# Window attention and MLP on one core: products of w1 on two engines, half-array transposes for the second chunk, and a fixed order of the first ones

## The chip, the core and the metric

The kernel runs on one core of a Trainium2 chip. The metric is the device time of one execution in microseconds (us): 217.73 as the median of three runs (217.38 to 218.16). A core has TensorE (PE, which loads weights, PEld, and runs matmuls), VectorE (DVE), ScalarE (ACT), GpSimd (POOL) and SyncE (SP), each with an instruction queue of its own that it works off in order, and DMA engines that the queues of POOL, SP and ACT start. PE writes its results to PSUM, from where DVE and ACT evict them to SBUF.

## The reference

Four batches, eight heads, 768 positions, head size 64, model size 512, four sinks and a window of 128.

```python
keep = is_sink | in_window                       # pos < 4, or 0 <= row - col < 128
scores = np.where(keep, q @ k.T / 8, -1e9)
a = exp(scores - max); a = a / (a.sum(-1) + 1e-9)
x = (a @ v), heads side by side                  # (4, 768, 512)
xn = (x - mean) / sqrt(var + 1e-6) * g_ln
out = x + relu(xn @ w_ch1) @ w_ch2               # w_ch1 512x2048, w_ch2 2048x512
```

## The kernel before

The 3072 rows are 24 tiles of 128, two to a chunk, twelve chunks; three chunks make a batch. For each chunk k and q are loaded as bf16, turned so that the head size lies on the partitions (kT, qT), and multiplied to scores (in PSUM, bank pairs `pair`); ACT takes the exponential into `pe`, DVE applies the mask, PE multiplies with v and a column of ones (banks `one`), DVE divides by the sum of that column (`rec`, `x`), takes mean and variance (`bn`, `ag`, tile `st`) and subtracts the mean (`xc`). `xc` is turned into `xnt`. The MLP of a chunk (`mlp`, L1019 to L1080) has eight products `ph` with w1 (relu on ACT or DVE) and eight products `pc` with w2.

The order of the work is not written out. Every piece is an `Op` with a cost per engine, a due time (`prio`) and the buffers it reads, writes and holds; `Plan.run` (L114) places them one by one on the engine that would be done with them first, and hands out the PSUM and SBUF buffers as it goes. What a piece costs in the plan, and which engines it may use, thus decides the order on every engine. Where PE has a gap in the plan within the first 24 us, filler matmuls on constants are put in (L1137). The engines then run their lists, and wait for each other by semaphores.

The places that the change touches:

- **First chunk** (`chunk`, L645 to L680). k and q of the first 256 rows are loaded as f32 in halves of four heads (`natf`), cast to bf16 (`natc`, L663, on DVE or ACT), and turned by four matmuls with the identity each (L671), which write every second column of a PSUM bank; the two rows that a partition holds (index i) thus come out in order of rows. An eviction (L642, `evict`) copies 512 adjoining columns to kT or qT. There are four such groups: k and q of heads 0 to 3, k and q of heads 4 to 7.
- **Second chunk** (`by_pairs`, L578). k and q are loaded as bf16 (`natp`), 256 rows by 8 heads. Each is turned by 32 matmuls on quarters of the array (L599: 64 rows by 64 columns, 64 columns out), into two banks, one for each of the chunk's two tiles; each bank is evicted once, for one tile and all heads. Chunks 2 and 3 use the same function with k and q together (64 matmuls, bank pairs) and stay as they are; later chunks are turned by DMA.
- **Scores of the first tiles** (`attend_tile`, L727). For tiles 0 and 1 PE first writes the mask into the bank (L743), then adds the scores (L763); for tiles 2 and 3 the scores are L722, the sinks L777. An op `sc` waits for the evictions that hold its k and q.
- **Products of w1 with the LN weight** (L1098 to L1101). The first two chunks multiply `xnt` with the LN weight when it is evicted (L900). For the later ones w1 itself is multiplied, in place, when the first two chunks are done with a quarter of it: sixteen pieces of 128 x 512, on DVE.

The four quarters of w1 and of w2 come through POOL's DMA queue (L550, L553), in between the loads of v (L619, L637) and of k and q (L584). The first chunk's MLP has its products by tile (L1030), the others by chunk (L1037); the products with w2 are L1066.

## Time and profile before

| | |
|---|---|
| median of three runs | 217.73 us |
| the profiled execution | 219.54 us |
| its span | 218.0 us |
| mean granted clock of PE | 0.997 |
| busy: PE, PEld, DVE | 206.3, 144.6, 116.9 us |
| busy: ACT, POOL | 105.5, 112.0 us |
| moved by DMA | 28.09 MB, 129 GB/s |

The profile is one execution. Its page gives busy times by engine and by group of instructions and the chain of work that ended last; the trace behind it can be asked for a stretch of time. A line of the timeline reads: start and length in us, engine, line of the kernel, operation, tiles written and read, shapes, count, and in brackets how long the engine sat idle before it and who released it. "Issue" is time in which an engine waited for nothing that the profile shows. A line of the chain of waits has start, length and what it was. In a table of stretches each engine has its busy time and, in brackets, its instructions; the last columns are the clock that was granted to PE, the busy share of the DMA engines and GB/s.

### The profile page before, as it was taken

What the parts mean: (1) busy time and instruction counts of PE and PEld (TensorE: products, weight loads), DVE (VectorE), ACT (ScalarE), POOL (GpSimd) and SP (SyncE); (2) the same over time, 40 slices, a digit from 0 to 9 for tenths busy, and PEclk for the clock granted to TensorE, in tenths of its full rate; (3) what the DMA queues carried; (4) which work ended last, traced back from release to release, by engine and by line L of the source; (5) the groups of instructions that cost most, each with busy time, mean ns of one, the idle gap of its engine ahead of it and who ended that gap; (6) DMA issues with size and microseconds to landing.
All of it is one profiled execution on the core that took longest, in us unless ns stands there. A gap on an engine that the chain in (4) does not pass through costs nothing.

```text
span 218.0 us, 6719 instructions
## 1 busy us (share of the span) xinstructions
PE 206.3 (95%) x2773; PEld 144.6 (66%) x2795; DVE 116.9 (54%) x323; ACT 105.5 (48%) x170; POOL 112.0 (51%) x166
## 2 busy tenths in 40 slices
PE   7797999999999999999999999999999999999991
PEld 2566875664875875874865865865865865856761
DVE  4497875999535536446445456356265265262011
ACT  3785477154571572572562562562652652622600
POOL 7976642589873881871971980971970120120000
PEclk9999999999999999999999999999999999999998
DMA  5999999999999699699799799799999202203011
GB/s 158 185 190 207 192 207 189 161 168 127 200 164 138 116 127 148 83 175 155 123 134 144 117 141 156 105 149 140 110 144 139 75 0 75 72 3 114 6 53 61
DMA packets 104558, 28.09 MB, mean 129 GB/s; under 512 B 94788, under 2 KB 101576, under 8 KB 104520
## 3 DMA queue, kind: packets, MB, share of 16 engines
q0 software_dynamic: 69872, 13.18, 84.2%
q1 hardware_dynamic: 33592, 13.87, 33.3%
q10 hardware_dynamic: 1056, 0.52, 0.9%
q8 instruction: 24, 0.39, 0.8%
q14 instruction: 14, 0.11, 0.2%
HBM read 27.43 MB, written 6.29 MB: 155 GB/s over the span
## 4 chain that ended last, share of the span: by engine, by line
PE 84%; DVE 9%; DMA 2%; issue 2%; ACT 0%; SPq 0%; DVEq 0%
PE one L1066 36%; PE one L1037 34%; PE pair L971 3%; DMA natf<-in_k_dram 2%; PE one L944 2%; PE one L951 2%; PE one L1030 1%; DVE w L1100 1%; DVE st L872 1%; DVE x L864 1%; PE one L960 1%; PE one L979 1%; PE pair L722 1%; PE pair L743 1%; DVE xc L876 1%
## 5 line engine op out<-in xcount | busy, mean ns | idle before, releaser
L1066 PE MATMUL one<-w,h 128*128 128x512 bf16 (+1 forms) x378 | 84.5, 370 | 2.2 <-issue 1.6
L1047 ACT ACTIVATE h<-one 128x512 bf16<-128x512 f32 x93 | 55.6, 598 | 49.7 <-PE one L1037 44.9
L1037 PE MATMUL one<-xnt,w 128*128 128x256 bf16 x704 | 79.3, 273 | 0.0
L1037 PEld LDWEIGHTS <-w 128*128 128x128 bf16 x704 | 68.6, 98 | 10.4
L1066 PEld LDWEIGHTS <-h 128*128 128x128 bf16 x400 | 37.3, 98 | 39.6
L989 ACT ACTIVATE pe<-pair 128x768 bf16<-128x768 f32 x36 | 27.2, 808 | 43.1 <-PE pair L971 43.1
L637 POOL DMA_DIRECT2D vn<-in_v_dram x59 | 38.7, 701 | 9.8 <-DMA w<-in_moe_w_ch_dram 6.8
L881 POOL TENSOR_SCALAR st<-st 128x1 f32<-128x1 f32 x24 | 8.9, 371 | 65.5 <-DVE st L874 65.1
L1012 DVE RECIPROCAL rec<-one 128x4 f32<-128x4 f32 x36 | 6.4, 177 | 62.0 <-PE one L960 50.6
L1074 DVE SCALAR_TENSOR_TENSOR ot<-one,st,x 128x512 f32<-128x512 f32 (+1 forms) x25 | 18.1, 726 | 12.9 <-PE one L1066 7.9
L882 POOL TENSOR_TENSOR st<-st,mhalf 128x1 f32<-128x1 f32 x24 | 17.0, 707 | 2.0
L872 DVE BATCH_NORM_STATS2 st<-x 128x6 f32<-128x512 bf16 x24 | 16.7, 694 | 0.8
L1014 DVE TENSOR_TENSOR x<-one,rec 128x256 bf16<-128x256 f32 x36 | 15.3, 424 | 1.2
L695 POOL DMA_DIRECT2D nat<-in_k_dram x16 | 14.9, 933 | 1.7 <-DMA natp<-in_q_dram 1.0
L695 POOL DMA_DIRECT2D nat<-in_q_dram x16 | 14.3, 907 | 0.0
L994 DVE TENSOR_TENSOR pe<-pe,band 128x768 bf16<-128x768 bf16 x24 | 12.2, 551 | 0.0
L1030 PE MATMUL one<-xnt,w 128*128 128x128 bf16 x128 | 8.3, 219 | 1.3 <-issue 1.0
L876 DVE TENSOR_SCALAR xc<-x,st 128x512 bf16<-128x512 bf16 x24 | 9.0, 374 | 0.9
L971 PE MATMUL pair<-qT,kT 64*64 64x128 bf16 (+1 forms) x528 | 9.2, 204 | 0.0
L944 PEld LDWEIGHTS <-pe 128*128 128x128 bf16 (+1 forms) x144 | 6.3, 97 | 3.3 <-DVE pe L994 0.8
L1030 PEld LDWEIGHTS <-w 128*128 128x128 bf16 x128 | 7.4, 98 | 1.6 <-issue 1.4
L769 ACT ACTIVATE pe<-pair 128x1024 bf16<-128x1024 f32 (+1 forms) x8 | 7.1, 916 | 2.5 <-PE pair L722 2.0
(109 smaller groups left out, 163.0 us busy)
## 6 DMA issues: line engine op xcount, KB each, us to landing
out_dram<-ot SPq DMA_DIRECT2D x23, 256.0 KB
w<-in_moe_w_ch_dram POOLq DMA_DIRECT2D x8, 512.0 KB, 14.4
nat<-in_k_dram POOLq DMA_DIRECT2D x16, 128.0 KB, 4.5
nat<-in_q_dram POOLq DMA_DIRECT2D x16, 128.0 KB, 5.7
vn<-in_v_dram POOLq DMA_DIRECT2D x44, 32.0 KB, 5.6
vn<-in_v_dram POOLq DMA_DIRECT2D x15, 64.0 KB, 5.8
natp<-in_k_dram POOLq DMA_DIRECT2D x3, 256.0 KB, 14.3
vn<-in_v_dram POOLq DMA_DIRECT2D x6, 128.0 KB, 9.6
```

What stands on the lines that cost most here:

```text
L637: P.op(f"vld{t}_{i}", {"POOL": (0.8, 0.85)}, prio + 0.001 * i, lambda e, p0=p0, n=n, hs=hs, src=src: G.dma_start(m.t[p0:p0 + n, hs, 0:64], ...
L695: lambda e, nat=nat, ap=ap: G.dma_start(nat.t, ap), writes=[nat], dma=SW, after=gate(c))
L872: P.op(f"bn{t}", {"DVE": fix(0.60)}, d + 0.12, lambda e: V.bn_stats(st.t[:, 8:14], x.t), reads=[x], writes=[st, mv])
L882: G.tensor_tensor(st.t[:, 16:17], st.t[:, 17:18], mhalf, op=ALU.pow)),
L971: nc.tensor.matmul(pps[u].t[64 * g:64 * g + 64, h2, col + c0:col + c0 + n], lhsT=kt.t[rs, hp, k0:k0 + 64], rhs=qT.t[rs, hp, q0:q0 + n], st ...
L989: nc.scalar.activation(pes[j].t.rearrange("p a b -> p (a b)")[:, 0:768].rearrange("p (a b) -> p a b", a=2), pps[j].t[:, :, 0:384], AF.Exp, ...
L1014: P.op(f"x{t - 1}{u}", {"DVE": dve(256)}, d + 0.051 + 0.002 * u, lambda e, u=u, rc=rc, pv=pv: V.tensor_tensor(x.t[:, 256 * u:256 * u + 256 ...
L1030: nc.tensor.matmul(ph.t[:, 128 * s:128 * s + 128], lhsT=w1[u // 2][:, j, 128 * s:128 * s + 128], rhs=xnt.t[:, j, 128 * (u % 2):128 * (u % ...
L1037: nc.tensor.matmul(ph.t[:, 256 * s:256 * s + 256], lhsT=w1[ht // 4][:, j, 128 * (ht % 4):128 * (ht % 4 + 1)], rhs=xnt.t[:, j, :], start=j ...
L1047: nc.scalar.activation(hb.t, ph.t, AF.Relu)
L1066: nc.tensor.matmul(pc.t[:, 0:wd], lhsT=(h1[2 * s + i].t[:, 128 * ii:128 * ii + 128] if by_tile else h1[ht // 2].t[:, 256 * (ht % 2) + 128 ...
L1074: V.scalar_tensor_tensor(ot.t[:, sl], in0=pc.t[:, 0:wd], scalar=st.t[:, 16:17], in1=x.t[:, sl], op0=ALU.mult, op1=ALU.add),
```

## The change

Four edits. (1) The first chunk's transposes write adjoining columns of the bank (one block of 128 for each i), and the eviction reads with a stride to bring rows into order; their planned cost goes from 0.3 to 0.23. (2) The second chunk's k and q (`whole`) are turned by 16 matmuls on half the array (128 rows by 64 columns, 128 columns out); the two banks now hold heads 0 to 3 and heads 4 to 7 of both tiles, an eviction is for four heads and both tiles, and `tile_of` says so; planned cost 0.45 instead of 0.28. The sink scores wait for both halves of q. (3) The scores of tile 0's first half wait until the last of the four transposes is issued, and the scores of tile 1's first half until those of tile 0's second half are. (4) The sixteen products of w1 and the LN weight may run on ACT too.

The lists of instructions of the two kernels show what follows from it. POOL and SP keep theirs. On ACT and DVE eight products of w1 each: of the four of a quarter, DVE has 3, 1, 1 and 3 and ACT 1, 3, 3 and 1; those of the second quarter that ACT has stand before the relu of the second chunk's fifth product, the others between relus and evictions up to the first exponential of the second batch. All four casts of the first chunk are on ACT, and three of the four evictions on DVE (before: two casts and three evictions on ACT). On PE the first scores stand behind the fourth group of transposes, tile 0's second half before tile 1's first; the products of tile 0 with v stand ahead of a mask; one product with w1 of the first chunk stands behind half of tile 3's product with v; there are five more fillers ahead of the second chunk's transposes and two fewer later. PE has 58 instructions fewer. Elsewhere only the numbers of PSUM buffers are permuted.

```diff
@@ -562,7 +562,7 @@
     xnt_b = [Buf(f"xnt{c}", "xnt") for c in range(NC)]
     xnt_t = [Buf(f"xnt_t{t}") for t in range(NT)]
 
-    tile_of, scores, trs = {}, {}, {}
+    tile_of, scores, scored, trs = {}, {}, {}, {}
 
     def early(t):
         return 0.5 + 0.8 * t
@@ -577,7 +577,7 @@
 
     def by_pairs(c, what, d):
         b, R = c // RC, c % RC
-        nats, pts = [], []
+        nats, pts, whole = [], [], len(what) == 1
         for nm, src, T, ld in what:
             nat = Buf(f"{nm}n{c}", "natp")
             ap = src[b, :, 256 * R:256 * R + 256, :].rearrange("h (p i) d -> p h (i d)", i=2)
@@ -593,24 +593,31 @@
             for nat, pt in zip(nats, pts):
                 for hp in range(HP):
                     for i in range(2):
+                        for h2 in range(2) if whole else ():
+                            nc.tensor.matmul(pt[hp // 2].t[64 * h2:64 * h2 + 64, 256 * (hp % 2) + 128 * i:256 * (hp % 2) + 128 * i + 128],
+                                             lhsT=nat.t[:, 2 * hp + h2, i, :], rhs=ident, start=True, stop=True, skip_group_check=True)
+                        if whole:
+                            continue
                         for h2 in range(2):
                             for r in range(2):
                                 rs, cs = slice(64 * r, 64 * r + 64), slice(64 * h2, 64 * h2 + 64)
                                 nc.tensor.matmul(half(pt, r)[cs, hp, i, :], lhsT=nat.t[rs, 2 * hp + h2, i, :],
                                                  rhs=ident[rs, rs], start=True, stop=True, skip_group_check=True)
-        o = P.op(f"tr{what[0][0]}{c}", pe(0.28 * len(what)), d, tr, reads=nats + [Bc["ident"]], hold=[w[2] for w in what],
-                 writes=[x for pt in pts for x in pt], mode="q")
+        o = P.op(f"tr{what[0][0]}{c}", pe(0.45 if whole else 0.28 * len(what)), d, tr, reads=nats + [Bc["ident"]], hold=[w[2] for w in what],
+                 writes=[x for pt in pts for x in pt], mode="h" if whole else "q")
         for (nm, src, T, ld), pt in zip(what, pts):
             for r in range(2):
                 t, done = 2 * c + r, Buf(f"{nm}T{2 * c + r}")
                 if c == 1:
                     trs[t] = [o]
                 evict(f"ev{nm}{t}", d + 0.05 + 0.02 * r, 512,
-                      lambda pt=pt, r=r: half(pt, r).rearrange("p h i m -> p h m i"),
-                      lambda T=T, r=r: T.t[:, :, 128 * r:128 * r + 128].rearrange("p h (m i) -> p h m i", i=2),
+                      lambda pt=pt, r=r: pt[r].t.rearrange("p (h i m) -> p h m i", h=2, i=2) if whole else
+                      half(pt, r).rearrange("p h i m -> p h m i"),
+                      lambda T=T, r=r: (T.t[:, 2 * r:2 * r + 2, :] if whole else T.t[:, :, 128 * r:128 * r + 128]
+                                        ).rearrange("p h (m i) -> p h m i", i=2),
                       [pt[-1 if len(pt) == 1 else r]], [T, done], fp=True)
                 for hh in range(2):
-                    tile_of[nm, t, hh] = done
+                    tile_of[(nm, 2 * c + hh, r) if whole else (nm, t, hh)] = done
 
     def load_v(t, prio):
         b, r = t // RB, t % RB
@@ -665,16 +672,16 @@
                              reads=[part], hold=[src], writes=[nat])
 
                         def tr(e, pt=pt, nat=nat):
-                            pb = pt.t.rearrange("p (h m i) -> p h m i", h=2, i=2)
+                            pb = pt.t.rearrange("p (h i m) -> p h i m", h=2, i=2)
                             for hp in range(2):
                                 for i in range(2):
-                                    nc.tensor.matmul(pb[:, hp, :, i], lhsT=nat.t[:, i, 2 * hp:2 * hp + 2, :], rhs=ident,
+                                    nc.tensor.matmul(pb[:, hp, i, :], lhsT=nat.t[:, i, 2 * hp:2 * hp + 2, :], rhs=ident,
                                                      start=hp + i == 0, stop=True, skip_group_check=True)
-                        o = P.op(f"tr{nm}{hh}", pe(0.3), d + 0.02 + 0.01 * hh, tr, reads=[nat, Bc["ident"]], hold=[T], writes=[pt])
+                        o = P.op(f"tr{nm}{hh}", pe(0.23), d + 0.02 + 0.01 * hh, tr, reads=[nat, Bc["ident"]], hold=[T], writes=[pt])
                         trs[0], trs[1] = trs.get(0, [o]), [o]
                         evict(f"ev{nm}0{hh}", d + 0.05 + 0.01 * hh, 512,
-                              lambda pt=pt: pt.t.rearrange("p (h c) -> p h c", h=2),
-                              lambda T=T, hh=hh: T.t[:, 2 * hh:2 * hh + 2, :], [pt], [T, done], fp=True)
+                              lambda pt=pt: pt.t.rearrange("p (h i m) -> p h m i", h=2, i=2),
+                              lambda T=T, hh=hh: T.t[:, 2 * hh:2 * hh + 2, :].rearrange("p h (m i) -> p h m i", i=2), [pt], [T, done], fp=True)
                         for t in range(2):
                             tile_of[nm, t, hh] = done
             else:
@@ -763,7 +770,8 @@
                             nc.tensor.matmul(pp.t[:, h2, col:col + 128], lhsT=kt.t[rs, hp, ks], rhs=qT.t[rs, hp, own],
                                              start=t >= PAR["pm"] and col == 0, stop=True, skip_group_check=True)
             done = Buf(f"sd{t}{j}")
-            P.op(f"sc{t}_{j}", pe(0.2 if t > 1 else 0.25 if t else 0.13), d + 0.1 + 0.1 * j, sc, reads=need[j], **(
+            first = trs[1] if (t, j) == (0, 0) else [scored[0, 1]] if (t, j) == (1, 0) else []
+            scored[t, j] = P.op(f"sc{t}_{j}", pe(0.2 if t > 1 else 0.25 if t else 0.13), d + 0.1 + 0.1 * j, sc, reads=need[j], after=first, **(
                 {"rw": [pp], "writes": [done]} if t < PAR["pm"] else {"writes": [pp, done]}),
                  hold=[kT, qT, kprev, pb], mode="q" if t > 1 else "r")
             P.op(f"ex{t}_{j}", {"ACT": act(1024 if t else 512)}, d + 0.11 + 0.1 * j, lambda e, pp=pp, pb=pb, at_j=at_j: nc.scalar.activation(
@@ -776,7 +784,7 @@
                 for hp in range(HP):
                     nc.tensor.matmul(pp_s.t[32 * hp:32 * hp + 32, 0:128], lhsT=kts_b[0].t[:, hp, :],
                                      rhs=qT.t[:, hp, own], start=True, stop=True, skip_group_check=True)
-            P.op(f"sk{t}", pe(0.21), d + 0.15, sk, reads=[tile_of["q", t, 0], kts_b[0]], writes=[pp_s], hold=[qT, ps], mode="c")
+            P.op(f"sk{t}", pe(0.21), d + 0.15, sk, reads=[tile_of["q", t, 0], tile_of["q", t, 1], kts_b[0]], writes=[pp_s], hold=[qT, ps], mode="c")
             P.op(f"sx{t}", {"ACT": act(128)}, d + 0.16, lambda e: nc.scalar.activation(
                 ps.t[:, own], pp_s.t[:, 0:128], AF.Exp, scale=scale), reads=[pp_s], writes=[ps])
 
@@ -1096,8 +1104,9 @@
         if c == PAR["x_by_dma"] - 1:
             for s in range(4):
                 for j in range(NDM):
-                    P.op(f"w1g{s}{j}", {"DVE": fix(0.26)}, 16.0 * c + PAR["w1g"] + 2 * s + 0.1 * j,
-                         lambda e, s=s, j=j: V.tensor_scalar_mul(w1[s][:, j, :], w1[s][:, j, :], gt[:, j:j + 1]),
+                    P.op(f"w1g{s}{j}", {"DVE": fix(0.26), "ACT": act(512)}, 16.0 * c + PAR["w1g"] + 2 * s + 0.1 * j,
+                         lambda e, s=s, j=j: V.tensor_scalar_mul(w1[s][:, j, :], w1[s][:, j, :], gt[:, j:j + 1]) if e == "DVE" else
+                         nc.scalar.mul(w1[s][:, j, :], w1[s][:, j, :], gt[:, j:j + 1]),
                          reads=[Bw1[s], Bc["gt"]], writes=[Bw1g[s]], after=last_use[s])
 
     def guard(e):
```

## The prediction

> **What bounds the kernel now.** Durations come from one profiled execution of 219.54 us: a span of 218.0 and 1.54 around it. The runs shown have a median of 217.73 (217.38 to 218.16), 1.81 lower, so I work out a difference in span and take it off the median. The table of stretches comes first (busy time and count of each engine per stretch), because it says where TensorE (PE) is not full; above it stands the page's line of totals.
>
> ```profile
> PE 206.3 (95%) x2773; PEld 144.6 (66%) x2795; DVE 116.9 (54%) x323; ACT 105.5 (48%) x170; POOL 112.0 (51%) x166
> ```
> ```profile
> core 0: us, PE busy (x) PEld busy (x) DVE busy (x) ACT busy (x) POOL busy (x), PEclk, DMA share, GB/s
> 0.00:16.46 16.46, 13.69 (x222) 7.68 (x222) 10.50 (x44) 11.12 (x18) 13.77 (x22) 1.00 1.36 178
> 16.46:17.50 1.04, 0.00 (x0) 0.00 (x0) 0.46 (x2) 1.00 (x2) 1.04 (x3) 1.00 1.25 205
> 17.50:26.25 8.75, 7.85 (x147) 7.11 (x147) 7.88 (x19) 3.89 (x6) 5.28 (x9) 1.00 1.43 198
> 26.25:53.00 26.75, 26.21 (x401) 17.31 (x404) 21.87 (x67) 14.04 (x24) 15.91 (x24) 1.00 1.46 173
> 53.00:214.00 161.00, 158.59 (x2010) 112.47 (x2022) 76.08 (x193) 75.47 (x122) 75.95 (x112) 1.00 1.15 114
> ```
> From 53 to 214 us PE is 98% busy at full clock; the change touches no work there, and the two instruction lists agree there on every engine but for the numbers of PSUM buffers. So the end moves by what PE gains before 53 us. Three places can give: the head up to 26 us, the 1.04 us in which PE ran nothing, and the half microsecond missing in 26 to 53. The chain of waits, in order of time, names what stood there:
>
> ```profile
> 6.58 0.95 DVE natc L663
> 7.58 0.61 PE one L671 x4
> ...
> 9.47 1.03 ACT pe L769
> ...
> 15.62 0.83 PE one L1030 x13
> 16.46 1.05 issue
> ...
> 17.95 0.69 DVE h L1049
> ...
> 25.68 0.53 DVE xc L876
> ...
> 26.25 0.40 PE one L889 x4
> ```
> Up to 16.5 us the chain hops between casts, transposes, exponentials and normalisation. From 17.95 to 26.2 it is VectorE's queue (DVE) in one run of 8.3 us: from the first relu, through normalising tiles 1 to 3, to the last x minus mean; PE's transpose at 26.25 waits for that. What started the run late is the stop of 1.05 us, with three matmuls of the first w1 product still to come.
>
> **First chunk (dense transposes, their order).** Rows of the timeline:
>
> ```profile
> 4.86 1.14 ACT L663 CAST natc<-natf 128x512 bf16<-128x512 f32 x2 [1.21 <-DMA natf<-in_k_dram]
> ...
> 8.23 0.58 ACT L642 CAST kT<-one 128x512 bf16<-128x512 f32 x1 [0.91 <-PE one L671]
> ...
> 8.99 0.69 DVE L642 CAST qT<-one 128x512 bf16<-128x512 f32 x1 [1.14 <-PE one L671]
> ...
> 10.54 0.69 DVE L642 CAST kT<-one 128x512 bf16<-128x512 f32 x1 [0.53 <-PE one L599]
> ...
> 11.30 0.18 DVE L862 RECIPROCAL rec<-one 128x4 f32<-128x4 f32 x1
> ...
> 13.88 0.40 PE L889 MATMUL one<-ident,xc 128*128 128x128 bf16 x4
> ...
> 14.21 0.24 PE L777 MATMUL one<-qT,kts 128*32 128x128 bf16 x4
> ```
> The new list puts all four casts on ScalarE (ACT) and three of the four evictions on DVE. The third cast starts at 6.58, when its data lands, and takes some 0.6 (1.14 for two) where DVE's took 0.95: the third transpose starts at 7.25, not 7.58. Four transposes into every second column take 0.61; four into adjoining columns (L889) take 0.40, and I take that for the dense ones. The fourth cast ends near 7.75, its transposes near 8.2, and ACT's eviction (0.58) near 8.8, where before DVE's ended at 8.99 + 0.69 = 9.68: 0.9 earlier. The eviction now reads with a stride. L642's evictions of the second chunk (10.54 among them) do so already, at 0.69 on DVE as at 8.99: nothing.
>
> The wait that holds the first scores back until all four transposes are issued starts them at 8.1 as before (in the old list they stood just before the fourth group), for their k and q are evicted by 7.4 (two of 0.69 on DVE, behind transposes done near 5.9). Behind the waiting scores on PE stand only the gain's transpose and fillers. The second half of tile 0 now precedes tile 1, so tile 1's exponential starts 0.25 later than 9.47, but ACT is through all three at 10.75, not 10.98. The five fillers added here stand where PE waits for a cast or an eviction anyway.
>
> **Second chunk (half-array matmuls).** 32 matmuls of 64x64 take 0.45 to the last result (10.04 to 10.49); 16 of 64x128 replace them, for k and for q. No row has a stationary of 128 rows by 64 columns. Bounds: one after the other at the 0.06 that a 128-column matmul steps by (15.62 above, 13 in 0.83) they cost 16 x 0.06 + 0.2 for the last to come through = 1.15; four beside each other like the quarter-array matmuls of L777 (0.24 for all four), 4 x 0.06 + 0.2 = 0.45. I take pairs side by side, 8 x 0.06 + 0.2 = 0.7: 0.25 more, twice. In exchange DVE is free for k's first half at 9.7 instead of 10.54, so the reciprocal of 11.30 starts at 10.4 (0.9 earlier). The second time the q tile's landing and ACT's queue leave less: tile 1's x minus mean ends near 16.2 instead of 16.96. I carry **0.75** for the head, with 0 and 0.9 as ends (serial matmuls cost 0.45 twice, nearly all of it).
>
> **The stop at 16.46.** Nothing that PE reads was missing: the 13 matmuls before it use the same tiles. The instruction queue is the one thing that fits:
>
> ```profile
> 17.50 0.17 PEld L1030 LDWEIGHTS <-w 128*128 128x128 bf16 x3 [1.22 <-issue]
> 17.50 0.34 PE L1030 MATMUL one<-xnt,w 128*128 128x128 bf16 x3 [1.05 <-issue]
> ```
> ```profile
> q8 instruction: 1, 0.02, 5.3%
> ```
> PE stopped after 222 loads and 222 matmuls (first stretch above). Of the DMA view's windows, the one from 15.1 to 16.2 has the one packet shown of queue 8 (16 KB); those from 12.4 to 15.1 and 16.2 to 21.1 have none. So I read it as PE having run out of instructions until a block arrived. The change leaves the data loads' order alone but takes 56 instructions from PE ahead of this point: in the new list instruction 444 is no longer inside the first w1 product but in the second half of tile 3's scores, which I put at 17.45. If the block comes at 17.50 as before, the stop is gone: **1.05** off the chain, and even a late block would stop PE beside DVE's run.
>
> The Trainium skill, "Runtime: NRT & Kernel Launch", section "Instruction fetch mechanics", says that an engine's sequencer fetches the next block of 256 instructions while it executes the current one, and that this is mostly hidden; this speaks against a stop of this size, and is my first rival.
>
> **What caps both.** 0.75 + 1.05 = 1.80 at the first relu meets loads that do not move. Issues of w1 and w2 (DMA view, one row each for the windows 9.9:10.0, 15.1:16.2 and 16.56:17.2), and PE's uses:
>
> ```profile
> w<-in_moe_w_ch_dram POOLq DMA_DIRECT2D x1, 512.0 KB, 15.0
> ```
> ```profile
> w<-in_moe_w_ch_dram POOLq DMA_DIRECT2D x1, 512.0 KB, 14.4
> ```
> ```profile
> w<-in_moe_w_ch_dram POOLq DMA_DIRECT2D x1, 512.0 KB, 16.1
> ```
> ```profile
> 26.49 1.95 PE L1030 MATMUL one<-xnt,w 128*128 128x128 bf16 x32
> ...
> 31.64 1.03 PE L1066 MATMUL one<-w,h 128*128 128x512 bf16 x3
> ...
> 33.29 2.76 PE L1066 MATMUL one<-w,h 128*128 128x512 bf16 x12
> ```
> The last quarter of w1 lands at 9.9 + 15.0 = 24.9 and is used at 26.49; the first of w2 at 15.7 + 14.4 = 30.1, used at 31.64; the second at 16.5 + 16.1 = 32.6, used by the third group of four, 33.29 + 4 x 0.23 (2.76 for 12) = 34.2. Slack is 1.5 each time. Tile 3's part of DVE's run also waits for PE, so I bring it in 1.4 earlier: **1.4** at 26.25, not 1.8.
>
> **Products of w1.** Chain of waits, and rows of the timeline:
>
> ```profile
> 48.83 2.23 DVE w L1100 x6
> ...
> 51.13 0.70 DVE w L1100 x2
> 51.82 0.94 DVE pe L994 x2
> ```
> ```profile
> 40.13 0.60 ACT L1047 ACTIVATE h<-one 128x512 bf16<-128x512 f32 x1 [1.79 <-PE one L1037]
> ...
> 49.48 1.51 ACT L989 ACTIVATE pe<-pair 128x768 bf16<-128x768 f32 x2 [1.54 <-PE pair L971]
> ...
> 52.34 0.20 PE L944 MATMUL one<-vn,pe 64*128 64x65 bf16 x1
> ...
> 52.81 0.30 PE L944 MATMUL one<-vn,pe 64*128 64x65 bf16 x7 [0.27 <-DVE pe L994]
> ```
> Eight products stand in front of the masks for which PE waits at 52.34 to 52.81. The new list has four there on DVE, so the masks come 1.5 earlier, bound then by ACT's exponentials (done near 51): the wait goes, **0.4**. ACT takes eight of the sixteen, at most 0.6 each (its cast of the same size), 4.8 in the 12.7 that it is idle between 26.25 and 53. Three of them stand right before the relu of 40.13, which it otherwise reaches with 1.79 to spare, so nothing is priced there; without that cover each holds the relu, and at worst PE, back by up to 0.6. Next late after the masks is nothing: PE is then full.
>
> **Sum**: 1.4 + 0.4 = 1.8 off the span, 218.0 to 216.2; from the median, **215.9**.
>
> **Rivals.** (1) The stop stays with the w1 product, because it was no missing instruction block: the relu gains 0.75 to 0.85, less than the loads allow, and with 0.4 that is 1.2: 216.5. This is the case that the Trainium skill speaks for on its page "Runtime: NRT & Kernel Launch". For it: no row names a releaser. Against: the one packet just before PE resumes. Chance 0.16. (2) The head's gain is lost in the loads: were the w quarters to land 1.4 later than here, or the half-array matmuls serial and the block late, only the 0.4 is left: 217.3. For it: a slack of 1.5 on three loads in a row; against: their issues are untouched. Chance 0.10. (3) Slower, by this row of the page's list of queues:
>
> ```profile
> q8 instruction: 24, 0.39, 0.8%
> ```
> PE, ahead of its instruction stream, stops at the next two blocks too: with 24 packets for its 5568 instructions a block is about 230, so near instructions 670 and 900. Each stop like the one seen costs 1.05 and falls where PE is the bound; the first has moved and not gone. That is 0.75 + 0.4 gained and 2.1 lost: 218.7. It decides if PE comes to those instructions before the block's packet plus the 1.4 us that the first took. For it, PE is 1.4 us earlier; against it, each block begins some 56 instructions later in the work. Chance 0.08.
>
> **How the numbers follow.** The forecast has 0.66. Its own ends: 2.5 off (head 0.9, loads earlier, 215.2) and 1.3 off (serial matmuls, 216.4). With rival 1 and 0.4 for a part of its wait kept, the range is 215.2 to 216.9, leaving out rivals 2 and 3 (0.18). A difference of 0.3% (0.65 us) is about what a measurement of this kernel can tell from none: faster 0.66 + 0.16 = 0.82, same 0.10, slower 0.08.
>
> **What would show it.** Right: the first w1 product in one piece, its relu near 16.3; no empty 1.04 us of PE before 26 us, or one beside busy DVE; the last w1 product of the first chunk near 25.1; no wait for the masks near 51; the second chunk's 16 transposes within 0.7. Wrong: an issue wait of a microsecond in a w1 product, PE waiting for w near 25, 30 or 33, or ACT's products ahead of a relu for which PE waits.

## The result, and the profile after

Lines of the changed kernel stand 7 to 8 below those of before (L889 is L897, L1030 is L1038, L1037 is L1045, L1066 is L1074, L1078 is L1086, L944 is L952, L994 is L1002; the half-array transposes are L597).

| | before | after |
|---|---|---|
| median of 21 runs each | 218.69 us (217.38 to 219.80) | 217.62 us (216.47 to 218.42) |
| ratio, 95% interval | | 0.9939 (0.9918 to 0.9959) |
| the same two, once more (35 and 12 runs) | 218.61 | 217.84, ratio 0.9971 (0.9947 to 0.9995) |
| profiled execution, span | 219.54, 218.0 | 217.13, 215.5 |

By the two ratios the change makes the kernel 0.3 to 0.6% faster (0.6 to 1.3 us); 0.83% (1.8 of 217.73) was forecast. The forecast of 215.9, range 215.2 to 216.9, did not hold the time. A part of that is its base: the three runs shown before had a median of 217.73, the 21 runs 218.69. Taken off the longer base, 1.8 would have given 216.9, still below 217.62: the gain itself was put too high as well.

The table of stretches of the changed kernel, to be held against the first one of before (busy time and count of each engine, then PE's clock):

```profile
0.00:16.46 16.46, 13.38 (x197) 7.68 (x197) 11.13 (x45) 11.29 (x18) 13.54 (x22) 1.00 1.36 178
16.46:17.50 1.04, 0.67 (x14) 0.66 (x15) 1.04 (x3) 0.81 (x2) 1.04 (x3) 1.00 1.25 205
17.50:26.25 8.75, 8.24 (x157) 7.50 (x154) 7.77 (x22) 3.98 (x7) 5.72 (x10) 1.00 1.43 198
26.25:53.00 26.75, 26.75 (x430) 17.01 (x428) 20.40 (x62) 19.70 (x33) 16.13 (x25) 1.00 1.56 178
```

PE works in the stretch that was empty, and from 26.25 to 53 it is full (26.75 of 26.75, before 26.21), while ACT has 5.7 us more and DVE 1.5 less. The chain of waits of the changed kernel, from the first MLP on:

```profile
14.20 0.69 DVE xnt L908
...
16.42 0.35 DVE xc L884
16.77 0.52 DVE h L1057
...
24.50 0.37 DVE xc L884
...
24.91 0.40 PE one L897 x4
```

The stop is gone from the chain; it now runs through DVE's queue without a break, and the relu (`h`) waits behind tile 1's x minus mean (`xc`), no longer for PE. Tile 3's transposes start at 24.91 instead of 26.25. Near 53 us stands the first w1 product of the third chunk, the first that needs the multiplied w1 (the expectations below call it the second chunk's). Its rows in the timelines of before and after:

```profile
55.37 0.82 PE L1037 MATMUL one<-xnt,w 128*128 128x256 bf16 x6
```
```profile
53.52 0.71 PE L1045 MATMUL one<-xnt,w 128*128 128x256 bf16 x5
```

It comes 1.85 us earlier, and the last `ot` of the kernel starts 1.86 earlier too (211.80 against 213.66). So these two profiles agree with the sum of 1.8, and the runs do not. Two profiles are two draws; the experiments show what was drawn.

### The profile page after: what moved, and what is told of

Its sections match the earlier page's. It is cut to its first block, busy times and chain, and to the rows that moved or that the text cites. A ratio compares the mean times of both kernels' runs of the same rounds, so it can differ in the third digit from the quotient of the medians.

```text
span 215.5 us, 6681 instructions
## 1 busy us (share of the span) xinstructions
PE 207.7 (96%) x2766; PEld 144.2 (67%) x2766; DVE 114.7 (53%) x315; ACT 110.0 (51%) x178; POOL 111.4 (52%) x166
## 4 chain that ended last, share of the span: by engine, by line
PE 89%; DVE 5%; DMA 2%; ACT 1%; issue 1%; SPq 0%; DVEq 0%
PE one L1074 40%; PE one L1045 36%; PE pair L979 3%; DMA natf<-in_k_dram 2%; PE one L952 2%; PE one L959 2%; PE one L968 1%; DVE st L880 1%; DVE xnt L908 1%; PE one L987 1%; PE one L1038 1%; DVE x L872 1%; PE pair L604 1%; PE pair L729 1%; DVE pe L780 1%
## 5 line engine op out<-in xcount | busy, mean ns | idle before, releaser
L1074 PE MATMUL one<-w,h 128*128 128x512 bf16 (+1 forms) x400 | 87.4, 371 | 0.0
L1045 PE MATMUL one<-xnt,w 128*128 128x256 bf16 x704 | 79.3, 273 | 0.0
L1045 PEld LDWEIGHTS <-w 128*128 128x128 bf16 x704 | 68.6, 98 | 10.4
L1074 PEld LDWEIGHTS <-h 128*128 128x128 bf16 x400 | 37.3, 98 | 39.6
L889 POOL TENSOR_SCALAR st<-st 128x1 f32<-128x1 f32 x24 | 8.5, 355 | 61.8 <-DVE st L882 61.2
L1022 DVE TENSOR_TENSOR x<-one,rec 128x256 bf16<-128x256 f32 x36 | 15.3, 425 | 1.2
L1002 DVE TENSOR_TENSOR pe<-pe,band 128x768 bf16<-128x768 bf16 x24 | 12.2, 551 | 0.0
L884 DVE TENSOR_SCALAR xc<-x,st 128x512 bf16<-128x512 bf16 x24 | 8.5, 353 | 0.9
L952 PEld LDWEIGHTS <-pe 128*128 128x128 bf16 (+1 forms) x144 | 6.2, 97 | 2.9 <-issue 0.8
L1038 PE MATMUL one<-xnt,w 128*128 128x128 bf16 x128 | 8.1, 219 | 0.0
L979 PEld LDWEIGHTS <-kT 64*64 64x64 bf16 x528 | 7.2, 108 | 0.4 <-ACT w L1109 0.4
```

The source lines that it names most:

```text
L979: nc.tensor.matmul(pps[u].t[64 * g:64 * g + 64, h2, col + c0:col + c0 + n], lhsT=kt.t[rs, hp, k0:k0 + 64], rhs=qT.t[rs, hp, q0:q0 + n], st ...
L1002: V.tensor_mul(at_s, at_s, band[j] if r > 1 else edge[r][j].unsqueeze(1).to_broadcast([128, 4, 192]))
L1022: P.op(f"x{t - 1}{u}", {"DVE": dve(256)}, d + 0.051 + 0.002 * u, lambda e, u=u, rc=rc, pv=pv: V.tensor_tensor(x.t[:, 256 * u:256 * u + 256 ...
L1045: nc.tensor.matmul(ph.t[:, 256 * s:256 * s + 256], lhsT=w1[ht // 4][:, j, 128 * (ht % 4):128 * (ht % 4 + 1)], rhs=xnt.t[:, j, :], start=j ...
L1074: nc.tensor.matmul(pc.t[:, 0:wd], lhsT=(h1[2 * s + i].t[:, 128 * ii:128 * ii + 128] if by_tile else h1[ht // 2].t[:, 256 * (ht % 2) + 128 ...
```

## The experiments

All ratios are to the kernel before, run beside on the same chip, with their 95% intervals.

**The two kernels again, unchanged.** For before:

> The kernel before, unchanged, for a second profile and more times. Theory A (PE runs out of instructions at its 444th and waits for a block): the stop of about 1.05 us stands again after 222 loads and 222 matmuls, at 16.2 to 17.5 us, with the packet of queue 8 before it. Theory B (the stop belongs to the first w1 product, by chance or by its data): another place or length, or none. Theory C (the times of one kernel fall into two groups about 1.2 us apart because the stop is there in some executions only): no stop if this execution's time is 218.4 or less, a stop if it is above 219. Ratio to the kernel before 1.00.

> The kernel before, unchanged, for a third profile. New theory: TensorE stops after 222 loads and 222 matmuls, until 5.4 to 5.9 us after it passed its 188th instruction, whatever the length of the stop that this gives (1.04 and 0.22 so far). Ratio 1.000.

Ratios 0.9988 (0.9962 to 1.0015) and 1.0002 (0.9976 to 1.0029). Their chains of waits where PE stops, b_again first:

```profile
15.68 0.83 PE one L1030 x13
16.51 0.22 issue
16.74 0.35 PE one L1030 x3
```
```profile
15.22 0.83 PE one L1030 x13
16.05 0.44 issue
16.49 0.35 PE one L1030 x3
```

The place is the same to the matmul, the length is not: 1.05, 0.22 and 0.44 us (and 0.93 in only_w1 below, whose PE does the same work up to there). Tile 3's transposes start at 26.25, 25.33 and 25.07. The profile that the forecast was worked out from had the longest of the three stops.

The changed kernel again:

> The changed kernel once more, for a second profile of it. If the 1.85 us between the two traces at 53 us is what the change is worth, its second chunk's first w1 product starts at 53.5 again; that of before, taken twice, was 55.37 and 54.60, the difference being the length of the stop (1.04 and 0.22). Ratio 0.994.

Its third chunk's first w1 product starts at 53.67, tile 3's transposes at 25.08. Over three profiles of before (55.37, 54.60, 54.36: mean 54.78) and two of after (mean 53.60) the gain there is 1.18 us, 0.54% of 218.6. That lies between the two measured ratios.

**Half-array matmuls alone, and cut in two.**

```diff
+                        for h2 in range(2) if whole else ():
+                            nc.tensor.matmul(pt[hp // 2].t[64 * h2:64 * h2 + 64, ...128 columns], lhsT=nat.t[:, 2 * hp + h2, i, :], rhs=ident, ...)
```
```diff
+                        for cc in (0, 64) if whole else ():
+                            for h2 in range(2):
+                                nc.tensor.matmul(...64 columns, rhs=ident[:, cc:cc + 64], ...)
```

> The kernel before with the half-array transposes of the second chunk alone: 64 instructions fewer on PE and two or so more fillers' worth, so that instruction 444 lies in the scores of tile 3. A: no empty microsecond in the first w1 product; the relu of that product near 16.8 instead of 17.95, the third tile's transpose near 25.2 instead of 26.25, ratio 0.995. B: the stop stays in the first w1 product, ratio 1.000 to 1.002 (0.2 us lost in each transposition).

> As only_half, but each half-array matmul of 128 columns in two of 64 columns: same work, same plan and order, 64 more instructions on PE ahead of the first w1 product, so that instruction 444 is again its 14th matmul. A: the stop is back there, about 1 us, until about 17.5; ratio 1.000, 1.0 us slower than only_half. B: as only_half to 0.2 us.

only_half: 0.9952 (0.9923 to 0.9981), no stop, tile 3's transposes at 24.86. half_split: 1.0005 (0.9977 to 1.0034), with the stop back; its chain of waits:

```profile
15.36 0.89 PE one L1039 x14
16.25 0.64 issue
16.89 0.27 PE one L1039 x2
```

The same work in 64 more instructions, and the gain is gone. What the half-array matmuls bring is their number. They also bring all that was gained ahead of tile 3: no_w1 (below), which has edits 1 and 3 besides, has tile 3's transposes at 24.89, no earlier than only_half's 24.86.

**First chunk's edits alone** (dense transposes and the fixed order, edits 1 and 3):

```diff
-                            pb = pt.t.rearrange("p (h m i) -> p h m i", h=2, i=2)
+                            pb = pt.t.rearrange("p (h i m) -> p h i m", h=2, i=2)
...
+            first = trs[1] if (t, j) == (0, 0) else [scored[0, 1]] if (t, j) == (1, 0) else []
```

> The kernel before with the dense first transposes and their fixed order alone (quarter-array transposes and w1 products on VectorE as before). Instruction 444 is the tenth matmul of the first w1 product. A: the head up to the second tile's x minus mean comes 0.4 to 0.8 earlier, but PE stops in the first w1 product until about 17.5 as before, so the relu gains 0.2 at most and the ratio is 0.998 to 1.000. B: the whole head's gain arrives, ratio 0.997.

0.9987 (0.9960 to 1.0014). Tile 0's transposes are 0.39 earlier than in before's profile (13.49 against 13.88; b_third, unchanged, has 13.47), and PE then waits longer at the same count. Its chain:

```profile
15.23 0.67 PE one L1031 x10
15.90 1.26 issue
17.15 0.51 PE one L1031 x6
```

**Products of w1 alone, and the change without them.**

```diff
-                    P.op(f"w1g{s}{j}", {"DVE": fix(0.26)}, ...
+                    P.op(f"w1g{s}{j}", {"DVE": fix(0.26), "ACT": act(512)}, ...
```

> The kernel before with the products of w1 and the gain also on ScalarE, nothing else. Theory A (the stop goes with the count of TensorE's instructions, and the products are a gain of their own): the stop after 222 loads and 222 matmuls stays in the first w1 product, 0.2 to 1.3 us long; the wait for the masks near 52 (0.4 us) is gone; ratio to before 0.998 (0.4 of 218.6). Rival B (the products cost ScalarE what they save VectorE): a wait before a relu near 40 us takes the place of the masks' wait, ratio 1.000.

> The changed kernel without the products on ScalarE (edits 1 to 3). Theory A with the products worth 0.4: the wait for the masks is back near 51 and the second chunk's first w1 product starts 0.4 later than in the changed kernel (53.9 against 53.52); ratio to before 0.996. Rival B: products worth nothing, ratio 0.994.

0.9982 (0.9957 to 1.0007) and 0.9967 (0.9934 to 1.0000). The products with v for which the masks had been late, in the timelines of only_w1 and of no_w1:

```profile
52.00 0.30 PE L944 MATMUL one<-vn,pe 64*128 64x65 bf16 x8
```
```profile
51.37 0.20 PE L952 MATMUL one<-vn,pe 64*128 64x65 bf16 x1 [0.29 <-DVE pe L1002]
51.83 0.17 PEld L952 LDWEIGHTS <-pe 64*128 64x128 bf16 x7 [0.38 <-DVE pe L1002]
51.84 0.30 PE L952 MATMUL one<-vn,pe 64*128 64x65 bf16 x7 [0.27 <-DVE pe L1002]
```

With the products shared, eight run in one piece; without them PE waits twice. The intervals can't tell 0.4 from nothing, the traces can: from tile 3's transposes to the third chunk's first w1 product it is 28.60 to 28.73 us in the eight profiles with products on ACT (mean 28.63), and 29.05 to 29.51 in the nine without (mean 29.26). The products are worth **0.63**, more than the 0.4 that the expectations had.

**Is it the count?** Two kernels that move the 444th instruction and nothing else: before without its five later fillers, and the changed kernel with its five first fillers cut in eight.

```diff
-        if n > 0 and room > 0.3:
+        if n > 0 and room > 0.3 and cold:
```
```diff
                 for i in range(-s):
-                    nc.tensor.matmul(o[1][:, 0:o[0]], lhsT=junk[:, 0:128], rhs=junk[:, 0:o[0]], ...)
+                    for p in range(8 if o[0] == 512 else 1):
+                        cols = slice(64 * p, 64 * p + 64) if o[0] == 512 else slice(0, o[0])
+                        nc.tensor.matmul(o[1][:, cols], lhsT=junk[:, 0:128], rhs=junk[:, cols], ...)
```

> The kernel before without its five filler matmuls after 5.6 us (10 instructions fewer on TensorE, no other work touched). The first w1 product has then ended 4 instructions before the 444th, which is in tile 1's transposes. Theory A (TensorE runs out of instructions at the 444th): the w1 product is in one piece and its relu near 16.7, and tile 1's transposes are what stops, until 16.8 to 17.5; ratio 0.996 to 0.999. Rival C (something in the w1 product itself holds TensorE there, such as its weights): the product stops with three matmuls left, as before, and the ratio is 0.999 to 1.000.

> The changed kernel with its five first filler matmuls of 512 columns each cut in eight of 64 (35 matmuls and 35 loads more at 1 to 3 us, where TensorE waits for the first data; everything behind them unchanged). The 444th instruction is then in the first w1 product again. Theory A: a stop of 0.2 to 1.3 us inside the first w1 product, tile 3's transposes 0.3 to 1.1 later than in the changed kernel (24.91), ratio to before 0.996 to 0.999. Rival D (the half-array matmuls gain by themselves, and the stop is of another kind): no stop, tile 3's transposes near 24.9, ratio 0.994.

> The kernel of a_fill8 once more, whose profile had a granted clock of 0.85 from 5 to 16.2 us. At full clock the first w1 product starts near 15.4 and TensorE comes to its 444th instruction after 6 of the 16 matmuls, near 15.8. Theory A: it stops there until 16.7 to 17.5, as in the other kernels, 0.9 to 1.7 us; ratio 0.995 to 0.998. Rival D: no stop; ratio 0.994.

b_less: the w1 product is in one piece, and PE pauses between the second and the third of tile 1's transposes, again behind 222 loads and 222 matmuls:

```profile
16.63 0.28 PE one L889 x2
16.92 0.13 issue
17.05 0.30 PE one L889 x2
```

The time, though, is 219.83, ratio 1.0061 (1.0029 to 1.0093), which neither theory had; more of it below. a_fill8: 0.9951 (0.9927 to 0.9975), and a_fill8_b, the same kernel at full clock, 0.9954 (0.9931 to 0.9977). In a_fill8_b 222 loads and 222 matmuls end ahead of the seventh load of the first w1 product, and nothing stops there:

```profile
15.32 1.07 PE L1038 MATMUL one<-xnt,w 128*128 128x128 bf16 x16
16.70 0.40 PE L897 MATMUL one<-ident,xc 128*128 128x128 bf16 x4 [0.31 <-DVE xc L884]
```

So the theory that the place in the list decides fell. What differs is when the packet of queue 8 came. The DMA view of a_fill8_b from 12.9 to 13.2 us, and that of the changed kernel from 15.1 to 15.3:

```profile
q8 instruction: 1, 0.02, 19.5%
```
```profile
q8 instruction: 1, 0.02, 29.5%
```

The 70 early instructions brought it two microseconds forward (13.06 against 15.19), and PE's 95th load as much (9.90 against 12.00). New theory: the block is asked for when PE is 256 instructions ahead of it (the 188th, its 95th load), takes a fixed time to come, and PE stops if it runs through the 256 faster. Two further runs, with the 256 in other work:

> The changed kernel with each half-array matmul cut in two of 64 columns (64 matmuls and loads more, same work). Its 188th instruction is then in tile 1's scores, near 11.2 us, and its 444th in the first w1 product after 9 matmuls, near 16.0: 4.8 us for 256 instructions. New theory (the block comes 5.4 to 5.9 after the 188th): a stop there of 0.6 to 1.1 us, resumed 16.6 to 17.1, tile 3's transposes near 25.4 instead of 24.91, ratio to before 0.996 to 0.999. Rival (neither place nor pace, a_fill8_b's missing stop being chance): no stop or one of any length, with no relation to 5.4 to 5.9 us.

> The kernel before with its five first filler matmuls each cut in eight of 64 columns (70 instructions more at 1 to 3 us, nothing else). Its 188th instruction is then in the first group of quarter-array transposes, near 10.1, and its 444th in tile 3's first scores, near 15.1 with no stop. New theory: the block comes at 10.1 + 5.4 to 5.9 = 15.5 to 16.0, so TensorE stops 0.4 to 0.9 us in those scores, and the first w1 product, now in one piece, ends near 17.0 instead of 17.86; ratio 0.996 to 1.000. Rival (the stop belongs to the w1 product): it stays there, with three matmuls left.

after_split is the changed kernel with the cut of half_split; b_fill8 is before with the cut fillers. Ratios 0.9984 (0.9958 to 1.0010) and 0.9982 (0.9954 to 1.0010). Their chains of waits, after_split first:

```profile
15.45 0.67 PE one L1040 x10
16.12 0.35 issue
16.47 0.51 PE one L1040 x6
```
```profile
14.38 0.29 PE pair L722 x14
14.67 0.64 issue
15.31 0.39 PE pair L722 x18
15.71 0.17 PE one L777 x4
15.88 1.01 PE one L1030 x16
```

In b_fill8 the stop has left the w1 product and stands in tile 3's scores, where the 444th instruction then is; the product is in one piece. after_split stopped 0.35, less than the 0.6 expected. Over all 17 profiles (packet times and counts of loads are from the trace's own records; the stop stands behind 444 to 446 instructions):

| | PE's 95th load to the first instruction of the block | packet on queue 8 to that instruction |
|---|---|---|
| nine that stop (before, b_again, b_third, only_w1, only_dense, half_split, b_less, b_fill8, after_split) | 5.35 to 6.13 us | 2.28 to 2.50 us |
| eight that don't (after, a_again, only_half, no_w1, a_less, w2_late, a_fill8, a_fill8_b) | 5.71 to 6.12 us | 2.54 to 3.11 us |

In the first row PE was there after 4.8 to 5.9 us and waited; in the second its own work took as long as the block, and no kernel got an instruction earlier than 2.28 us after the packet. That PE asks in steps of 256 the later packets show too: in all 17 profiles the first four came 2.7 to 3.9 us after PE's 95th, 223rd, 351st and 479th load, which are 128 loads and 128 matmuls apart (the second counted from the load behind the stop, where there is one). The time to come is not fixed, though: b_third's block came 0.43 sooner after the 95th load than before's (5.41 against 5.84), and its stop is shorter for that. The table also tells why b_again stopped so shortly: its load of q was late (a wait of 0.69 at 12.05, below), PE lost that time inside the 256, and got it back at the stop. What sets the 5.4 to 6.1 us was not tried; the DMA share in the tables of stretches is above 1.2 all that time.

**Where the head's gain went.** The changed kernel without its last five fillers, and the same with w2's loads issued later by POOL:

```diff
-        if n > 0 and room > 0.3:
+        if n > 0 and room > 0.3 and o.start < 9.5:
```
```diff
-    items = [(o.start, o.seq, o) for o in order]
+    late = {"w2ld0": 2.8, "w2ld1": 2.8, "w2ld2": 2.8, "w2ld3": 0.9}
+    items = [(o.start + late.get(o.name, 0.0), o.seq, o) for o in order]
```

> The changed kernel without the filler matmuls behind 9.5 us (two of 256 columns at 11.48, three more after the first w1 product). Theory E (in the changed kernel TensorE's own queue is the bound from 9.3 to 13.7, which is where the head's gain went): tile 0's transposes start at 13.4 instead of 13.69, tile 1's x minus mean ends 0.3 earlier than 16.77, ratio to before 0.9925. Rival F (VectorE's queue or the landing of the q load is the bound): tile 0's transposes stay at 13.6 to 13.7 or their copy at 14.2, ratio 0.994.

> The run a_less with the loads of w2's quarters issued by GpSimd behind tile 1's statistics instead of before (first issue near 16.9 instead of 15.76); every other engine's list is the same. Theory G (tile 1's x minus mean on VectorE is held while GpSimd begins to issue those loads): x minus mean starts near 16.1 as in a_less and takes 0.35 instead of 0.57, so it ends at 16.5, 0.2 earlier, and so do the relu and tile 3's transposes (24.65). Rival H (it is held by something else, or the relu by the first w1 product's end at 16.2): it ends at 16.7 again, tile 3's transposes at 24.86. The quarters of w2 land about a microsecond later, so the ratio is left open: 0.994 if PE has enough work before them, up to 0.998 if it waits for them near 30.

Ratios 0.9944 (0.9920 to 0.9968) and 0.9950 (0.9923 to 0.9977): neither beats the changed kernel. In a_less tile 0's transposes come at 13.41, as theory E had it, but tile 3's only at 24.86 (24.91). Its timeline, DVE and POOL, and then that of w2_late:

```profile
16.14 0.57 DVE L884 TENSOR_SCALAR xc<-x,st 128x512 bf16<-128x512 bf16 x1
...
15.76 2.36 POOL L553 DMA_DIRECT2D w<-in_moe_w_ch_dram  x3
```
```profile
16.25 0.35 DVE L884 TENSOR_SCALAR xc<-x,st 128x512 bf16<-128x512 bf16 x1
...
17.27 2.35 POOL L553 DMA_DIRECT2D w<-in_moe_w_ch_dram  x3
```

The x minus mean that begins 0.38 after POOL's first issue takes 0.57; with the issue behind it, it takes 0.35, as theory G had it. The other profiles make the pattern plain. In the first 60 us of all 17, an x minus mean takes 0.35 when it begins less than 0.2 us or more than 0.6 after POOL began to issue a load, but for one (in a_fill8, 0.92 beside a TENSOR_TENSOR of POOL). Of the 33 in between 30 are stretched, and 26 of them end 0.95 to 0.99 us after POOL began, whenever they started: for tile 1, b_third (begun 0.33 after, takes 0.63), b_less (0.44, 0.52), only_dense (0.48, 0.47), b_again (0.53, 0.42). So it is held until some 0.6 us after POOL's start, and what comes earlier in that window gains nothing. The Trainium skill ("SBUF — State Buffer", "Who interferes with whom") has such a rule: VectorE's tensor_scalar can take a port pair that it shares with GpSimd, and the later of the two blocks fully; the stretched rows agree, with 0.07 to 0.28 us lost by tile 1's. By the Trainium skill the first one keeps the pair for its whole instruction, and there the rows differ: POOL's issue of w2 takes 0.75, but holds an x minus mean until 0.6 only. w2_late's tile 3 is only 0.11 earlier than a_less's, half of what was expected, because its tile 0 was itself 0.12 later. Nor did w2 land later: its second quarter, issued 1.51 later than in a_less, landed at 32.46 (32.48).

**The end of the kernel.** b_less had its last `ot` at 212.58, 1.08 earlier than before, and yet ends later (span 218.4). In the trace's own records two of PE's last three instructions, parts of the final barrier, stand at 216.70 and 218.12, with a packet of queue 8 that began at 215.73, 2.39 before the second; in the other 16 profiles they are 0.15 to 0.20 apart. It fits that ten instructions fewer have moved the end of a block between them; no further run tests that. The end also varies by itself. From the end of the last `ot` to the end of the span it is 3.90, 4.22 and 3.17 us in the three profiles of before, so the second, with a stop of only 0.22, still took 219.09: the time of an execution does not tell whether PE stopped, and theory C of b_again fell. A part of it is SP's: the last issue of SP took 0.33 us in after and 0.63 in a_less, as these rows (three issues each, with the gaps between them) show, and the two spans differ by 0.7 (215.5 and 216.2) though the last `ot` differs by 0.06; where the rest comes from stays open:

```profile
209.07 3.57 SPq L1086 DMA_DIRECT2D out_dram<-ot  x3
```
```profile
209.01 3.87 SPq L1086 DMA_DIRECT2D out_dram<-ot  x3
```

## Why the prediction was right and wrong, by its steps

**The stop at 16.46: right in kind, too large in size.** It was missing instructions, it stood at the 444th, and with fewer instructions it went; half_split, after_split and b_fill8 show it by bringing it back or moving it. But 1.05 was one profile's length. Three profiles of before have 1.05, 0.22 and 0.44, a mean of 0.57; that the long one stood in the profile shown was chance. The rule from the Trainium skill that stood against it ("Runtime: NRT & Kernel Launch", "Instruction fetch mechanics") holds in its block of 256 instructions: the first four packets follow loads that are 256 instructions apart. It doesn't hold in being mostly hidden: in nine of 17 profiles PE stopped, for 0.13 to 1.26 us.

**The head: this step failed.** 0.75 was carried into the first relu; tile 1's x minus mean ended 0.18 earlier than in before's profile (16.77 against 16.95). The single prices were near: the third cast at 6.53, dense transposes 0.40 for four, ACT's eviction done at 8.79 (8.8 forecast), first scores at 8.10. But ACT was through its three exponentials at 11.18, not 10.75. Rows of the changed kernel (PE, and the eviction on DVE that waits for it), of before and of b_again:

```profile
9.34 0.51 PE L770 MATMUL pair<-qT,kT 64*128 64x128 bf16 x12 [0.48 <-ACT pe L777]
9.79 0.64 PE L597 MATMUL one<-ident,natp 128*64 128x128 bf16 x16
10.24 0.69 DVE L649 CAST kT<-one 128x512 bf16<-128x512 f32 x1 [0.96 <-PE one L597]
...
11.80 0.64 PE L597 MATMUL one<-ident,natp 128*64 128x128 bf16 x16
...
13.69 0.40 PE L897 MATMUL one<-ident,xc 128*128 128x128 bf16 x4
```
```profile
9.82 0.29 PE L763 MATMUL pair<-qT,kT 64*128 64x128 bf16 x4 [0.39 <-DVE gt L529]
10.04 0.45 PE L599 MATMUL one<-ident,natp 64*64 64x64 bf16 x32
...
11.98 0.45 PE L599 MATMUL one<-ident,natp 64*64 64x64 bf16 x32
```
```profile
12.05 0.44 PE L599 MATMUL one<-ident,natp 64*64 64x64 bf16 x32 [0.69 <-DMA natp<-in_q_dram]
```

The forecast let DVE evict k's first half at 9.7, when DVE would be free. DVE was free at 9.28 and waited 0.96 for PE's transposes: PE, held until 9.34 by ACT's exponential, had twelve score products ahead of them. PE was 0.48 earlier at 9.34 than before at 9.82, then full: each group of half-array matmuls took 0.19 more (0.25 forecast), and tile 0's transposes came 0.19 earlier. On the means of the profiles not even that is left: 13.77 in three of before (13.88, 13.95, 13.47) and 13.77 in two of the changed kernel (13.69, 13.85). The gain was read from DVE's reciprocal (10.85, 0.45 earlier) as if DVE were the chain there; it was PE's list, as a_less shows (two fillers fewer, tile 0's transposes 0.28 earlier). b_again says the same: its reciprocal was 0.69 earlier than before's (10.61), the load of q then held PE until 12.05, and tile 0's transposes came at 13.95 (13.88). Behind that stands the x minus mean that POOL's issue holds up: of a_less's 0.28 only 0.05 arrived at tile 3. So the relu came at 16.68 and not at 16.3, though the w1 product was in one piece; the last w1 product of the first chunk, at 25.15 (25.1 forecast), fits only through the cap below.

**The two were added.** 0.75 and 1.05 made 1.80, cut to 1.4 by the slack of the loads of w1 and w2. That cut hid the error: in the first pair of profiles 1.34 came off at tile 3, nearly all of it the stop. A gain inside the 256 instructions is paid back at the stop, as only_dense shows (13.49 at tile 0, a stop of 1.26, and tile 3 at 25.92, later than before's mean of 25.55). The loads capped nothing here: between 18 and 36 us PE waits for no load of w, in the changed kernel and in w2_late. But little was left: w1's last quarter landed at 24.53 and was used at 25.15, w2's second at 32.52 and was used, by the forecast's reckoning, near 32.9.

**Products of w1: right in kind, too small.** 0.4 was forecast, 0.63 measured. ACT took 0.74 for each instead of 0.6 (5.5 in all instead of 4.8), and hid that:

```profile
L1109 ACT ACTIVATE w<-w,gt 128x512 bf16<-128x512 bf16 x8 | 5.5, 736 | 0.0
```

**The sum.** On the means of the profiles: 0.55 at tile 3 (25.55 against 25.00) instead of 1.4, and 0.63 instead of 0.4, together 1.18 instead of 1.8. **The rivals.** The first gave 1.2 off, near the measured gain, by another mechanism: it kept the stop in the w1 product, which is gone. The third did not come: no later stop of PE stands in the chain. The second, at 217.3 the nearest to the measured time, had the head's gain lost, as it was, but in the loads of w, and the stop's gain with it; it was lost in PE's list instead, and the stop's gain was kept. Both numbers came near by luck.

## What to carry to other kernels

PE, running through its instructions faster than they were fetched, stopped where the block ended, whatever work stood there. So count the instructions up to an unexplained stop, look for a packet on the instruction queue ahead of it, and give the work of the block before it fewer instructions. A wait that has no releaser in the profile, and the median of three runs, are single draws: take a second profile of the unchanged kernel before such a wait becomes a term of a sum. Two gains in a row add up only if nothing between them has a clock of its own, as the fetch has and GpSimd's issue of a load.

## What the runs showed of the hardware

- A block of 256 instructions for PE came 5.35 to 6.13 us after PE had begun the block before it, and 2.28 to 2.50 us after the first packet on queue 8, in nine profiles in which PE stopped for it. Meanwhile the DMA share was 1.25 or more in the tables of stretches of before and after.
- The changed kernel with five early filler matmuls of 512 columns cut in eight each has the end of the block back in the first w1 product, and does not stop there (a_fill8_b): the packet came 2.13 us earlier, the 95th load 2.10. Before with the same cut still stopped, 0.64 us, in other work (b_fill8).
- Ten instructions fewer on PE made the kernel 0.6% slower (0.3 to 0.9%), with a gap of 1.42 us between two of PE's last instructions, in one profile; the packet 2.39 us before the second fits a late block.
- An x minus mean of 128x512 in bf16 on VectorE is held when it begins 0.2 to 0.6 us after GpSimd began to issue a load (30 of 33 cases), and takes up to 0.63 instead of 0.35 for tile 1.
- 16 matmuls of 128 rows by 64 columns, 128 columns out, in pairs on the two halves of the array: 0.64 us to the last result, against 0.45 for 32 on quarters.
